# Router logits of three row tiles in one group of matmuls, a second expert computed with seven block products, and shorter pauses in the last routing

## Chip, cores and metric

The kernel runs on one core of one Trainium2 chip. The metric is the device time of one execution in microseconds (us), lower is better. The engines are named as in the profile: PE is TensorE (PEld its weight loads), DVE is VectorE, ACT is ScalarE, POOL is GpSimd, SP is SyncE, whose instructions here only start transfers.

## What is computed

Block-sparse attention with 4 batches, 8 heads, 768 positions and 64 values a head, in blocks of 32 (each query block sees its neighbours, the first and the last block, and three sampled ones; the first and last query blocks see all). Its 3072 x 512 output is the input of a mixture of 8 experts, of which each row takes the best two:

```python
logits = x @ w_gate
noise_scale = np.log1p(np.exp(x @ w_noise))
noisy_logits = logits + noise_scale * noise
top2 = np.argpartition(-noisy_logits, 2, axis=1)[:, :2]
...                                  # top2_w: softmax over the two
h = np.maximum(x[mask] @ w1[e], 0.0) # w1[e] 512 x 1024
out[mask] += top2_w[mask, k, None] * (h @ w2[e])
```

## The kernel before

**Attention and router.** The attention is cut into steps; most of them ("G") handle one half of the heads of 128 query rows. `Attention.steps` writes the order by hand. A step issues the scores (L215), their row maximum on DVE (L250, L269), the transposes of the step before (L303, copied out by ACT, L305), the exponentials on ACT (L291), the product with the values for the step before that (L318), and its scaling on DVE. Two steps make one tile of 128 finished rows x; there are 24, in four groups of 6.

Between these, `step(n, spot)` puts the router's work. Two steps after a tile is done, `turn_rows` transposes it (L548, four transposes on PE, one DVE copy to `r_xT`); a step later `new_logits` multiplies it with the gate and noise weights (L560: the tile stands in the array, 16 columns stream past, copied out by DVE to `r_lc`, L562). Both stand at spot 1, right behind the L303 transposes, and share one PSUM tile, `pe`, with the routing's matmuls. When a group of 6 tiles has its logits, `Router.run` routes it: a generator of small DVE steps with two sorts of PE work, ranks (L635 to L639) and slot tables (L713). `background` takes steps from it. A `yield 2` ahead of PE work makes the following calls idle, as many as `FENCE` says.

**Experts.** There are nine units: units 0 and 1 are the two row sets of expert 0 (640 and 224 rows), units 2 to 8 are experts 1 to 7 with 816 rows. A unit is a first product and a second product (`mm2`). Weights and activations are split in two float16 parts, so each product is three matmuls. Units below `FAST` = 3 use `mm1` (L987): 8 blocks f, for unit 2 with 24 matmuls of 408 columns each. Units from `FAST` on use `fast1` (L1002): 7 block products in place of 8, 168 matmuls of 408 columns in place of 192. For that the weights need sums (`sums`, L838 and L857) and the transposed rows need sums too (`halves`, L880 and L898). These are made on DVE and ACT during the second product of the unit before (`coming`).

**The last routing** (rows of the last six tiles) runs inside unit 0: `mm1` calls `turn()` in the middle and at the end of each f, `mm2` in the middle and at the end of each chunk of 128 rows, and `turn` is `background(UB)` with `UB` = 20 and `FENCE` = [1, 2]. When it is done, `third()` gathers the rows of units 1 and 2 (L926 on POOL), transposes them by DMA (L942 on SP, to `xtb` for unit 1 and `xta` for unit 2). It goes one stage further per chunk of unit 0's second product.

Engines work in program order, each on its own queue, and wait for each other by semaphores.

## Time and profile before

| | us |
|---|---|
| median of 3 runs (864.75 to 867.81) | 866.12 |
| the profiled execution | 856.92 |
| its span, first to last instruction | 855.1 |
| attention and router, up to unit 0's first product | about 316 |
| unit 0 and unit 1 | 316 to 403.5 |
| unit 2 (expert 1), first product | 403.5 to 436.6 |

A row of the timeline gives start, duration, engine, line, operation, output and inputs, shapes, the count of merged instructions, and in brackets how long the engine sat idle before and what released it. "Issue" stands for a wait that the profile doesn't explain.

### The profile page before, as it was taken

Reading aid. Unit: us, or ns where it says so; the run is one execution under the profiler, and the core shown is the slowest. Engines: PE = TensorE matmul, PEld = TensorE weight load, DVE = VectorE, ACT = ScalarE, POOL = GpSimd, SP = SyncE. Lnnn points to the kernel's source line nnn. Section 1 sums busy time; section 2 is a strip of 40 time slices with the busy share of each in tenths; the row PEclk is TensorE's granted clock in tenths of the full one; section 3 lists DMA queues with packets and bytes.
Section 4 is the critical chain, followed back from the end, with each engine's and each line's share of the span. In section 5 each row is a group of like instructions: output and inputs, shape, how many; then the busy total and the mean of one; then the engine's idle time right before and its main releaser. Section 6 shows DMA issues by size and latency. Waiting matters only on the chain.

```text
span 855.1 us, 21866 instructions
## 1 busy us (share of the span) xinstructions
PE 791.1 (93%) x8889; PEld 483.4 (57%) x8889; DVE 549.3 (64%) x1122; ACT 372.6 (44%) x678; POOL 360.2 (42%) x555
## 2 busy tenths in 40 slices
PE   4899888889898878989999999999999999999996
PEld 2577676666676766548544544544544544544542
DVE  3555475756767845722558688678787786868741
ACT  2575464555565534301435445445435445435400
POOL 2534552542224520051317526537537546546431
PEclk9999898998998989999999999999999999999998
DMA  8856986695259898557845696695696695796221
GB/s 336 296 187 220 267 244 187 240 365 174 75 148 256 237 170 303 207 141 160 188 147 127 135 255 140 121 246 130 149 238 141 148 249 119 131 241 140 76 80 53
DMA packets 125021, 159.71 MB, mean 187 GB/s; under 512 B 66581, under 2 KB 83221, under 8 KB 124912
## 3 DMA queue, kind: packets, MB, share of 16 engines
q1 hardware_dynamic: 96400, 75.76, 32.6%
q0 software_dynamic: 20016, 57.47, 27.1%
q10 hardware_dynamic: 8496, 25.01, 9.3%
q8 instruction: 72, 1.18, 0.6%
q14 instruction: 37, 0.30, 0.1%
HBM read 117.30 MB, written 27.10 MB: 169 GB/s over the span
## 4 chain that ended last, share of the span: by engine, by line
PE 54%; DMA 1%; issue 1%; POOL 0%; DVE 0%; POOLq 0%
PE py L1083 26%; PE mb L1002 9%; PE ma L1002 6%; PE mc L1002 6%; PE ph L987 5%; PE py L1093 2%; DMA xtb<-xg 1%; PE py L1102 0%; DMA xg<-x_rows,gi 0%; POOL out_dram L1159 0%; DMA out_dram<-y,mt 0%; DVE y L1145 0%; PE pr L1114 0%; POOLq L1179 0%; POOLq L926 0%
## 5 line engine op out<-in xcount | busy, mean ns | idle before, releaser
L1133 POOL DMA_INDIRECT pv<-out_dram,gi x42 | 101.9, 2425 | 95.6 <-ACT pv L1127 49.3
L1002 PEld LDWEIGHTS <-wop 128*128 128x128 f16 x1008 | 98.6, 98 | 76.3
L1083 PEld LDWEIGHTS <-hh 128*128 128x128 f16 x768 | 74.5, 98 | 89.7 <-issue 2.5
L215 PE MATMUL s<-kv,q 64*32 64x192 f32 (+3 forms) x1920 | 95.9, 357 | 22.9 <-DMA kv<-in_k_dram 8.5
L305 ACT ACTIVATE t<-t 128x512 f32<-128x512 f32 (+1 forms) x120 | 63.0, 566 | 85.5 <-PE t L303 82.5
L205 POOL COPY kv<-kv 128x128 f32 x264 | 67.7, 305 | 52.9 <-issue 25.1
L1159 POOL DMA_INDIRECT out_dram<-pv,mt x42 | 51.8, 1233 | 89.2 <-DMA out_dram<-pv,mt 35.3
L1002 PE MATMUL mb<-tx,wop 128*128 128x408 f16 x432 | 83.3, 336 | 0.0
L215 PEld LDWEIGHTS s<-kv,q 64*32 64x32 f32 (+2 forms) x1920 | 52.6, 130 | 45.9 <-issue 16.6
L291 ACT ACTIVATE p<-s,nb 128x256 f32<-128x256 f32 x176 | 69.5, 477 | 19.3 <-DVE nb L269 13.8
L250 DVE TENSOR_REDUCE nm<-s 128x4 f32<-128x1024 f32 (+1 forms) x48 | 54.4, 1133 | 32.3 <-PE s L215 32.2
L1083 PE MATMUL py<-w2h,hh 128*128 128x512 f16 x192 | 72.8, 379 | 0.0
L1083 PE MATMUL py<-w1ha,hh 128*128 128x512 f16 x192 | 72.8, 379 | 0.0
L1083 PE MATMUL py<-w2l,hh 128*128 128x512 f16 x192 | 72.8, 379 | 0.0
L1083 PE MATMUL py<-w1la,hh 128*128 128x512 f16 x192 | 72.8, 379 | 0.0
L303 PE MATMUL t<-ident,p 128*128 128x128 f32 x448 | 69.1, 297 | 3.5 <-ACT t L305 3.5
L1083 PE MATMUL py<-w2h,hl 128*128 128x512 f16 x192 | 68.9, 379 | 0.0
L1083 PE MATMUL py<-w1ha,hl 128*128 128x512 f16 x192 | 68.8, 379 | 0.0
L303 PEld LDWEIGHTS t<-ident,p 128*128 128x128 f32 x448 | 51.2, 148 | 28.0 <-issue 15.7
L1007 ACT ACTIVATE hh<-us 128x408 f16<-128x408 f32 x48 | 26.1, 543 | 91.8 <-DVE us L1023 91.8
L926 POOL DMA_INDIRECT xg<-x_rows,gi x56 | 57.9, 1033 | 15.9 <-issue 15.0
L1083 PEld LDWEIGHTS <-hl 128*128 128x128 f16 x384 | 37.6, 98 | 45.3
(213 smaller groups left out, 1465.1 us busy)
## 6 DMA issues: line engine op xcount, KB each, us to landing
wraw<-in_moe_w_dram SPq DMA_DIRECT2D x64, 512.0 KB, 5.3
vb<-in_v_windows_dram ACTq DMA_DIRECT2D x28, 390.0 KB, 6.3
vb<-in_v_windows_dram ACTq DMA_DIRECT2D x14, 520.0 KB, 4.9
kv<-in_v_dram SPq DMA_DIRECT2D x4, 1560.0 KB, 17.8
q<-in_q_dram SPq DMA_DIRECT2D x12, 512.0 KB, 8.0
kv<-in_k_dram SPq DMA_DIRECT2D x8, 768.0 KB, 11.1
out_dram<-zero ACTq DMA_DIRECT2D x8, 768.0 KB, 5.1
x_rows<-x SPq DMA_DIRECT2D x20, 256.0 KB, 3.4
```

Source lines behind the costliest of these rows:

```text
L205: nc.gpsimd.tensor_copy(KG[:, j, :, 32 * s:32 * s + 32], KT[:, :, bass.ds(offs[3 * j + s], 32)])
L215: mm = lambda out, l, r, pos: nc.tensor.matmul(out, l, r, start=True, stop=True, tile_position=pos)
L250: red = lambda out, x: nc.vector.tensor_reduce(out, x, axis=AX.X, op=ALU.max, negate=True)
L291: self.nc.scalar.activation(p[:, 256 * u:256 * u + 256], S[:, a, 256 * r:256 * r + 256], AF.Exp, bias=nb[:, u:u + 1], scale=0.125)
L303: self.nc.tensor.transpose(T[i][:, c:c + P], p[:, i * w + c:i * w + c + P], self.ident)
L305: self.nc.scalar.activation(t[:, i * w:(i + 1) * w], T[i][:, 0:w], AF.Copy)
L926: g = nc.gpsimd.indirect_dma_start(out=self.xg[0:m, c], out_offset=None, in_=self.x_dram[0:nr], in_offset=bass.IndirectOffsetOnAxis(ap=r[" ...
L987: nc.tensor.matmul(ph[:, b, 0:m], w[wt][:, kb, fs], r["xt"][:, kb, a, o:o + m], start=i == 0, stop=i == last)
L1002: self.nc.tensor.matmul(bank[:, 0:H], w[:, h, o, k, cs], x(k, a), start=start and i == 0, stop=i == len(seq) - 1, skip_group_check=True)
L1083: nc.tensor.matmul(py, h[:, f, o], w[x][:, f, :], start=i == 0, stop=i == last)
L1133: g = nc.gpsimd.indirect_dma_start(out=y[0:m], out_offset=None, in_=self.out, in_offset=bass.IndirectOffsetOnAxis(ap=r["gi"][0:m, c:c + 1] ...
L1159: x = self.nc.gpsimd.indirect_dma_start(out=self.out, out_offset=bass.IndirectOffsetOnAxis(ap=self.st["u", u]["mt"][0:m, c:c + 1], axis=0) ...
```

## The change

Three things. (1) For 18 of the 24 tiles the logits of three tiles are computed at once: the weights, filled up to 32 columns, stand in the array, three copies side by side in column tiles, and the three transposed tiles stream past them (12 matmuls, 128 columns each). The result comes out transposed, is copied to `r_lt`, and is transposed back two steps later (`logits_rows`). Grouped are the first 15 tiles and tiles 18 to 20; tiles 15, 16, 17, 21, 22, 23 go one by one as before. All logits of the attention move from spot 1 to spot 2, behind the L318 products; `logits_rows` takes spot 1. (2) `FAST` is 2: unit 2 uses `fast1`. Its weights' sums are made in unit 0's second product, its rows' sums in unit 1. (3) `UB` is 10 and `FENCE` [1, 1] for the last routing, `third()` starts with whichever chunk of unit 0 finds it done, and unit 2's transposes take the chunks gathered first.

```diff
+    def logits_of_three(self, i, pl):
+        nc, KB = self.nc, self.D // P
+        for kb in range(KB):
+            for c in range(LG):
+                nc.tensor.matmul(pl[32 * c:32 * c + 32, 0:P], self.wgn[:, kb], self.xT[i - LG + 1 + c][:, kb],
+                                 start=kb == 0, stop=kb == KB - 1, tile_position=(0, 32 * c), skip_group_check=True)
+        for c in range(LG):
+            del self.xT[i - c]
+        nc.vector.tensor_copy(self.lt[0:32 * LG], pl[0:32 * LG, 0:P])
+
+    def logits_rows(self, i, pl):
+        nc, t = self.nc, i % self.T
+        nc.tensor.transpose(pl[:, 0:P], self.lt, self.ident)
+        nc.vector.tensor_copy(self.logit_tile(i)[:, t - LG + 1:t + 1],
+                              pl[:, 0:32 * LG].rearrange("p (t e) -> p t e", e=32)[:, :, 0:2 * E])
...
-        self.FAST = 3
+        self.FAST = 2
...
+    def grouped(i):
+        return i // T < B - 2 or i % T < T - LG
...
-    UB = 20
+    UB = 10
...
         if spot == 1:
+            logits_rows(n)
+            turn_rows(n)
+        if spot == 2:
             new_logits(n)
-            turn_rows(n)
...
-    FENCE[:] = [1, 2]
+    FENCE[:] = [1, 1]
...
         for i in range(ex.count(2)):
-            ex.xpose(2, i)
+            ex.xpose(2, (i + ex.count(1)) % ex.count(2))
...
     for u in range(nu):
         if u == 2:
             turns.close()
-            ex.open_third(hidden)
-        if u == ex.FAST:
             hidden.close()
...
-                ex.split_piece(*((0, 4 + f) if f < 4 else (1, f - 4)))
+                if f < 4:
+                    ex.split_piece(0, 4 + f)
...
-            if u == 2 and f < 4:
-                ex.split_piece(e, 4 + f)
+            if u == 1:
+                for i in {5: (0,), 6: (1,), 7: (2, 3)}.get(f, ()):
+                    ex.halves(2, i)
+            if u == 2 and f % 2 == 0:
+                ex.split_piece(e, 4 + f // 2)
...
-                if k < 4:
+                if k == n - 1:
+                    for _ in rest:
+                        pass
+                if k == 0:
+                    ex.sums_open(1)
+                for i in {0: ((0, 0),), 1: ((0, 1), (0, 2)), 2: ((0, 3), (1, 0)), 3: ((1, 1), (1, 2)), 4: ((1, 3),)}[k]:
+                    ex.sums(1, *i)
+                if k < 2:
                     ex.load_piece(1, 4 + k)
-            if u == 1:
-                for _ in range(3):
-                    next(rest, None)
+            if u == 1 and k == 0:
+                for i in range(6, 8):
+                    ex.load_piece(1, i)
+                for i in range(4, 6):
+                    ex.halves(2, i)
```

Where instructions move, three places. First PE in the attention, the step whose logits are those of the third tile; t are transposes, po the value products, s the next scores. Before:

```order
L303 MATMUL t_1419<-ident,p 128x128 x4
L560 MATMUL pe<-r_wgn,r_xT 128x16 x4
L318 MATMUL po<-va_87,t 32x65 x4
...
L318 MATMUL po<-vb_89,t 32x65 x4
L215 MATMUL s<-kv_85,q 128x64 x4
L215 MATMUL s<-kv_85,q 32x2x96 x16
```

Now (the new lines are `logits_of_three`, L576, and two steps later `logits_rows`, L585):

```order
L304 MATMUL t_1409<-ident,p 128x128 x4
L319 MATMUL po<-va_87,t 32x65 x4
...
L319 MATMUL po<-vb_89,t 32x65 x4
L576 MATMUL pe<-r_xT,r_wgn 32x128 x12
L216 MATMUL s<-kv_85,q 128x64 x4
...
L304 MATMUL t_1649<-ident,p 128x128 x4
L585 MATMUL pe<-r_ident,r_lt 128x128
L319 MATMUL po<-va_87,t 32x65 x4
```

The logits leave the place between the transposes and the value products; in two of three such steps nothing takes it, in the third the group stands behind the value products.

Second DVE around unit 1, whose first product leaves the hl pieces of 224 columns and whose outputs are the y rows behind them. Before:

```order
L1125 TENSOR_SCALAR y<-py,r_tab 128x512 x2
L993 SCALAR_TENSOR_TENSOR hl<-ph,hh 128x224 x8
L906 TENSOR_SCALAR mt<-r_tab 128x7
L912 TENSOR_SCALAR gi<-mt 128x7
L1125 TENSOR_SCALAR y<-py,r_tab 128x512
L1125 TENSOR_SCALAR y<-pr,r_tab 96x512
L993 SCALAR_TENSOR_TENSOR hl<-ph,hh 128x408 x2
```

Now (L895 are the rows' sums of unit 2, L1008 the hl, L1140 the y, L1038 the first addition of unit 2's `fast1`):

```order
L1008 SCALAR_TENSOR_TENSOR hl<-ph,hh 128x224 x6
L895 TENSOR_TENSOR xg<-xta 128x1632
L1008 SCALAR_TENSOR_TENSOR hl<-ph,hh 128x224
L895 TENSOR_TENSOR xg<-xta 128x1632
L1008 SCALAR_TENSOR_TENSOR hl<-ph,hh 128x224
L895 TENSOR_TENSOR xg<-xg 128x2x408 x4
L895 TENSOR_TENSOR tx<-xg,tx 128x1632 x2
L921 TENSOR_SCALAR mt<-r_tab 128x7
L927 TENSOR_SCALAR gi<-mt 128x7
L1140 TENSOR_SCALAR y<-py,r_tab 128x512
L1140 TENSOR_SCALAR y<-pr,r_tab 96x512
L1038 TENSOR_TENSOR r_xT<-mb,r_xT 128x408
```

The rows' sums of unit 2 stand between the last hl pieces of unit 1 and behind them.

Third POOL at unit 0's second product: the scatters of its chunks (out_dram<-y) and the gathers of units 1 and 2 (xg). Before:

```order
L1159 DMA out_dram<-y,mt 3072x512 x3
L926 DMA xg<-x_rows,gi 128x1024
L926 DMA xg<-x_rows,gi 96x1024
L926 DMA xg<-x_rows,gi 128x1024 x4
L926 DMA xg<-x_rows,gi 48x1024
```

Now:

```order
L1174 DMA out_dram<-y,mt 3072x512
L941 DMA xg<-x_rows,gi 128x1024
L941 DMA xg<-x_rows,gi 96x1024
L941 DMA xg<-x_rows,gi 128x1024 x4
L941 DMA xg<-x_rows,gi 48x1024
```

The gathers stand behind the first chunk's scatter instead of the third's.

## Rows read from the trace of the kernel before

**Rows 1.** The chain that ended last: start, us, what; pieces from 403 to 472.
```profile
403.50 33.12 PE ph L987 x192
...
470.51 1.04 PE ma L1002 x6
```
**Rows 2.** Timeline of PEld: a step with neither turn nor logits.
```profile
55.18 0.86 PEld L303 LDWEIGHTS t<-ident,p 128*128 128x128 f32 x8 [0.30 <-ACT p L291]
56.20 0.16 PEld L318 LDWEIGHTS po<-va,t 128*32 128x32 f32 x8 [0.17 <-issue]
```
**Rows 3.** The same view: steps with logits, with a turn, and the next transposes.
```profile
77.46 0.86 PEld L303 LDWEIGHTS t<-ident,p 128*128 128x128 f32 x8 [0.30 <-issue]
...
79.28 0.16 PEld L318 LDWEIGHTS po<-va,t 128*32 128x32 f32 x8
...
80.33 1.10 PEld L215 LDWEIGHTS s<-kv,q 64*128 64x128 f32 x40
81.73 0.86 PEld L303 LDWEIGHTS t<-ident,p 128*128 128x128 f32 x8 [0.30 <-ACT p L291]
...
83.19 0.16 PEld L318 LDWEIGHTS po<-va,t 128*32 128x32 f32 x8 [0.17 <-issue]
...
91.93 0.64 PEld L303 LDWEIGHTS t<-ident,p 128*128 128x128 f32 x6 [0.30 <-issue]
```
**Rows 4.** Timeline of ACT: last exponentials before the transposes at 81.73 and 91.93.
```profile
80.62 0.84 ACT L291 ACTIVATE p<-s,nb 128x256 f32<-128x256 f32 x2
...
89.84 1.20 ACT L291 ACTIVATE p<-s,nb 128x256 f32<-128x256 f32 x3
```
**Rows 5.** Timeline of PE: routing matmuls that waited for a logits copy.
```profile
171.62 1.60 PE L713 MATMUL pe<-r_val,r_hot 128*128 128x126 f32 x12 [0.87 <-DVE r_lc L562]
204.45 0.18 PE L635 MATMUL pe<-r_O,r_tri 128*128 128x48 f16 x1 [0.61 <-DVE r_lc L562]
292.17 1.60 PE L713 MATMUL pe<-r_val,r_hot 128*128 128x126 f32 x12 [1.44 <-DVE r_lc L562]
```
**Rows 6.** Timeline: the longest wait of PE inside value products.
```profile
131.47 0.33 PE L318 MATMUL po<-va,t 128*32 128x65 f32 x3 [4.12 <-issue]
```
**Rows 7.** Timeline of PE: unit 0's first product and first slot table.
```profile
340.34 0.70 PE L987 MATMUL ph<-xta,w1ha 128*128 128x320 f16 x4 [3.46 <-DVE hl L993]
...
353.11 1.60 PE L713 MATMUL pr<-r_val,r_hot 128*128 128x126 f32 x12 [1.04 <-DVE r_val L707]
354.55 0.38 PE L1083 MATMUL py<-w2h,hh 128*128 128x512 f16 x1
```
**Rows 8.** Timeline of DVE: the last routing's pieces in unit 0.
```profile
335.09 0.45 DVE L585 RECIPROCAL r_iw<-r_w 128x48 f32<-128x48 f32 x1
...
337.84 0.15 DVE L607 TENSOR_TENSOR r_dl<-r_mx 128x6 f32<-128x6 f32 x1
...
347.46 0.24 DVE L642 TENSOR_TENSOR r_A<-r_A,pr 128x96 f32<-128x96 f32 x1
...
350.28 0.17 DVE L684 TENSOR_SCALAR r_sl<-r_s 128x12 int32<-128x12 f32 x1
```
**Rows 9.** Timelines of PE, POOL and SP: unit 1's start, gathers and DMA transposes.
```profile
384.33 0.37 PE L987 MATMUL ph<-xtb,w1ha 128*128 128x224 f16 x2 [2.38 <-DMA xtb<-xg]
373.95 1.05 POOL L926 DMA_INDIRECT xg<-x_rows,gi  x1 [0.30 <-DVE gi L912]
375.30 0.97 POOL L926 DMA_INDIRECT xg<-x_rows,gi  x1 [0.31 <-issue]
390.14 10.29 SPq L942 DMA_TRANSPOSE xta<-xg  x7
```
**Rows 10.** Groups by line: shapes and count | busy us, mean ns of one | idle.
```profile
L880 DVE TENSOR_TENSOR xg<-xta 128x1632 f32<-128x1632 f16 x6 | 11.1, 1850 | 3.5 <-DMA xta<-xg 3.5
L880 DVE TENSOR_TENSOR xg<-xg 128x816 f32<-128x816 f32 x24 | 24.1, 1005 | 0.4
L898 ACT ACTIVATE tx<-xg 128x1632 f16<-128x1632 f32 x12 | 18.6, 1553 | 0.0
```

More of the change, by code (lines that the diff above doesn't have):

```diff
@@ L36 @@
 NSLOT = NV * OVC
+LG = 3
 BIGIDX = 1 << 20
@@ L484, in consts @@
         nc, pool, T, B, KB = self.nc, self.pool, self.T, self.B, self.D // P
-        wgn = self.wgn = pool.tile([P, KB, 2 * E], F32, name="r_wgn")
+        wgn = self.wgn = pool.tile([P, KB, 32], F32, name="r_wgn")
+        nc.vector.memset(wgn[:, :, 2 * E:], 0.0)
         nc.sync.dma_start(wgn[:, :, 0:E], w_gate.rearrange("(k p) e -> p k e", p=P))
-        nc.sync.dma_start(wgn[:, :, E:], w_noise.rearrange("(k p) e -> p k e", p=P))
+        nc.sync.dma_start(wgn[:, :, E:2 * E], w_noise.rearrange("(k p) e -> p k e", p=P))
         self.noise = pool.tile([P, B, T, E], F32, name="r_noise")
@@ L514, in tables @@
         nc.vector.tensor_scalar(self.tokf, self.tok, float(-BIGIDX), None, op0=ALU.add)
+        self.lt = pool.tile([P, P], F32, name="r_lt")
+        nc.vector.memset(self.lt, 0.0)
         self.tab = pool.tile([P, NV * NC, 2], F32, name="r_tab")
@@ L548, in turn, with logit_tile @@
             nc.tensor.transpose(pt[:, kb * P:(kb + 1) * P], xv[:, kb * P:(kb + 1) * P], self.ident)
-        self.xT[i] = self.pool.tile([P, self.D // P, P], F32, name="r_xT", bufs=2)
+        self.xT[i] = self.pool.tile([P, self.D // P, P], F32, name="r_xT", bufs=4)
         nc.vector.tensor_copy(self.xT[i].rearrange("p k r -> p (k r)"), pt)
+    def logit_tile(self, i):
+        b = i // self.T
+        if b not in self.lc:
+            self.lc[b] = self.pool.tile([P, self.T, 2 * E], F32, name="r_lc", bufs=2)
+        return self.lc[b]
     def logits(self, i, pl):
-        nc, T, KB = self.nc, self.T, self.D // P
-        b, t = divmod(i, T)
-        if t == 0:
-            self.lc[b] = self.pool.tile([P, T, 2 * E], F32, name="r_lc", bufs=2)
+        nc, KB = self.nc, self.D // P
         xT = self.xT.pop(i)
         for kb in range(KB):
-            nc.tensor.matmul(pl[:, 0:2 * E], xT[:, kb], self.wgn[:, kb], start=kb == 0, stop=kb == KB - 1,
+            nc.tensor.matmul(pl[:, 0:2 * E], xT[:, kb], self.wgn[:, kb, 0:2 * E], start=kb == 0, stop=kb == KB - 1,
                              skip_group_check=True)
-        nc.vector.tensor_copy(self.lc[b][:, t], pl[:, 0:2 * E])
+        nc.vector.tensor_copy(self.logit_tile(i)[:, i % self.T], pl[:, 0:2 * E])
+    def logits_of_three(self, i, pl):
+        nc, KB = self.nc, self.D // P
+        for kb in range(KB):
[10 more added lines that the diff above has]
+                              pl[:, 0:32 * LG].rearrange("p (t e) -> p t e", e=32)[:, :, 0:2 * E])
     def run(self, b, ps):
@@ L810, in open_first @@
     def open_first(self, e):
-        KB, F = self.KB, self.F
-        n = KB * F
-        if e == 0:
-            h, l = (self.wpa.tile([P, n], F16, name=x) for x in ("w1ha", "w1la"))
-        else:
-            both = self.sums_tile()
-            h, l = both[:, 0:n], both[:, n:2 * n]
-        view = lambda t: t.rearrange("p (k f) -> p k f", k=KB)
+        h, l = (self.wpa.tile([P, self.KB * self.F], F16, name=x) for x in ("w1ha", "w1la"))
+        view = lambda t: t.rearrange("p (k f) -> p k f", k=self.KB)
         self.wb[e] = {"w1h": view(h), "w1l": view(l)}
@@ L861, in sums @@
             self.sums_split(e, s, 0, top)
-            s3 = self.st["s3", e, s] = self.tsp.tile([P, 2, 256], F32, name="s3", bufs=2)
+            s3 = self.st["s3", e, s] = self.tsp.tile([P, 2, 256], F32, name="s3", bufs=1)
             tt(s3, a11, a21, ALU.subtract)
@@ L938, in xpose @@
         r = self.st["u", u]
-        if c == 0:
+        if "xt" not in r:
             pool, x = (self.xta, "a") if u % 2 == 0 else (self.xtb, "b")
@@ L1043, in fast1 @@
             mul(A, 0, plain(0, 0), True)
-            m = new("um", 2)
+            m = self.router.pool.tile([P, 4, P], F32, name="r_xT", bufs=4).rearrange("p k r -> p (k r)")[:, 0:H]
             nc.scalar.activation(m, A[:, 0:H], AF.Copy)
             mul(B, 2, mixed(1, 1), True)
-            s2 = self.router.pool.tile([P, 4, P], F32, name="r_xT", bufs=2).rearrange("p k r -> p (k r)")[:, 0:H]
+            s2 = self.router.pool.tile([P, 4, P], F32, name="r_xT", bufs=4).rearrange("p k r -> p (k r)")[:, 0:H]
             add(s2, B[:, 0:H], m)
@@ L1299, in turn_rows, with begin, logits_rows @@
             fresh.append((n + 1, i))
+    def grouped(i):
+        return i // T < B - 2 or i % T < T - LG
+    def begin(i):
+        if i % T == T - 1:
+            jobs.append(router.run(i // T, lambda: psum[0]()))
+            started[0] += 1
     def new_logits(n):
         while fresh and fresh[0][0] <= n:
+            i = fresh.pop(0)[1]
+            if grouped(i) and i % LG < LG - 1:
+                continue
             while router.held:
                 background()
-            i = fresh.pop(0)[1]
-            router.logits(i, psum[0]())
-            if i % T == T - 1:
-                jobs.append(router.run(i // T, lambda: psum[0]()))
-                started[0] += 1
+            if grouped(i):
+                router.logits_of_three(i, psum[0]())
+                turned.append((n + 2, i))
+            else:
+                router.logits(i, psum[0]())
+                begin(i)
+    def logits_rows(n):
+        while turned and turned[0][0] <= n:
+            while router.held:
+                background()
+            i = turned.pop(0)[1]
+            router.logits_rows(i, psum[0]())
+            begin(i)
     psum = [att.psum]
@@ L1434, in coming @@
         e = ex.units[u][1]
-        if u + 1 < ex.FAST:
-            return
         if k == 0:
```

4 lines of the change are left out of this document (1 added, 3 removed).

## Prediction

> **What bounds the kernel now.** I read the chain that ended last first. From 384.33 us, where unit 1 waits for a DMA transpose [rows 9], it follows PE alone to the last output, and unit 2's first product takes 33.12 us of it [rows 1]. So from there on PE's own work is the time. In the attention I read the timeline of weight loads, which shows when PE takes up each piece. PE goes from one piece to the next with no gap but a fixed 0.30 us ahead of each run of transposes [rows 2, 3]. So the attention is bound by PE as well, with two conditions. The gap is sometimes released by ACT's exponentials, so ACT is close behind. And PE has long waits that no instruction explains, 4.12 us at the longest [rows 6]; with it there are six above 1.4 us in the attention. They won't shrink because a matmul is gone.
>
> **Part 1, the logits.** From the start of a run of transposes to the value products a step takes 56.20 - 55.18 = 1.02 us with nothing between [rows 2], 79.28 - 77.46 = 1.82 with logits, and 83.19 - 81.73 = 1.46 with a turn [rows 3]. So one tile's logits cost 0.80 us and one transpose of 128 x 128 costs 0.44 / 4 = 0.11.
>
> A group of 12 new matmuls isn't in the trace. Nearest are the value products: 64 records (32 matmuls, each in a 32-column tile, four side by side) take 80.33 - 79.28 = 1.05 us [rows 3], so a set of four with 65 columns takes 0.131. Scaled to 128 columns that is 0.26, times four sets 1.03 us. The lower bound is the streaming of 128 columns at the transposes' rate, 0.86 / 8 = 0.108 us a record [rows 3], two records to a float32 matmul, four sets: 0.86 us. The upper bound is no overlap of the column tiles, 24 x 0.108 = 2.6 us. I take 1.0, since the value products show the overlap in this very form.
>
> Per group: two tiles' logits go (1.60), the third's 0.80 becomes 1.0, and a transpose comes (0.11): 1.3 us, times six groups 7.8. That the third tile's step gives no more is important. The transposes at 81.73, behind the third tile's logits, were released by ACT, whose exponentials ended at 80.62 + 0.84 = 81.46; behind the fourth's they ended at 91.04, 0.9 before the transposes at 91.93 [rows 3, 4]. So the steps that lose work have about 0.9 us of room on the side of ACT, those that get the group have little.
>
> Routing matmuls that waited for a logits copy, 0.87, 0.61 and 1.44 us [rows 5], no longer follow one. But three of them now follow a group, and must wait for DVE's copy of it: three times about 0.6, as in the middle one of these rows. That is +1.1 us. The wider copy and the copy back replace three copies of 0.17 us on DVE and hide beside PE.
>
> Two single tiles (17 and 21) now stand apart from the transposes, whose array shape they share. The trace shows 0.30 and 0.17 us at changes of shape [rows 2, 3], but none between logits and value products, so I count nothing. The Trainium skill, in "TensorEngine Tiling (Array Packing)", section Tiling Modes, says that every change of the tiling mode drains TensorE. By it the two tiles would cost 0.47 us each and the saving would be 0.9 smaller.
>
> Sum 8.9 us on PE. I take 6 of it (two thirds), because ACT, DVE and the unexplained waits give some back; bounds 2 (all that stands before a long wait is lost) and 9.
>
> **Part 2, the last routing.** Its calls pause less: one idle call behind a `yield 2` and not three, and at most ten steps at once. On PE the ranks (L635) come ahead of f = 5, the first slot table ahead of f = 7, the second in the middle of the first chunk. The wait of 3.46 us [rows 7] stays: PE needs hl of f = 3 and now also the ranks' inputs, and DVE makes both behind 2.75 us of routing from 335.09 on [rows 8], about 1 us for the rest; f = 5 starts near 340.5 as before (340.34) [rows 7]. The first table then is needed too early. DVE goes: hl of f = 4 until 344.2; L642 to L682, 350.28 - 347.46 = 2.8 us [rows 8], until 347.0; hl of f = 5 until 348.5; L684 until the table's inputs, 353.11 - 350.28 = 2.8 [rows 7, 8], until 351.3. PE has finished f = 6 at 348.8 (f = 5 and 6 take 8.3), so it waits 2.5 us, and the second product starts near 356.0 in place of 354.55 [rows 7]: 1.5 us lost. In return nothing waits later. The second product takes 27.2 us as before (five chunks and the second table) and ends at 383.2; the gathers start near 365 and not 373.95, and what took 384.33 - 375.30 = 9.0 us from the second gather to unit 1's start [rows 9] is over by 376. So the 2.38 us wait goes and unit 1 starts at about 383.2, 1.1 us earlier. After the 3.46 us wait f = 5 took 5.0 us where others take 3.3, at a granted clock below full; a second such fall would cost 1.7. I take +0.5, bounds -0.6 and +2.5.
>
> **Part 3, unit 2 by seven products.** 192 matmuls in 33.12 us become 168: 28 pieces of six at 1.035 us, 28.97 us [rows 1]. Gain 4.15. Its weights' sums lie on DVE and ACT in unit 0's second product, where DVE is idle most of the time, and cost nothing: at most 4.9 us of chain per chunk of 5.18. The rows' sums lie tighter. With t the end of f = 5 in unit 1 (f takes 1.17 us): hl of f = 5 until t + 1.1, a sum of 1.85 us [rows 10], hl of f = 6, a sum of 1.85, hl of f = 7 at t + 5.2. PE ends f = 7 at t + 2.3 and needs the last hl at t + 3.2, near the end of the first of four column blocks of the next product. It waits about 2 us, 2.3 with f = 6. Then four sums of 1.0 us, two ACT pieces of 1.55 and two DVE pieces of 1.86 [rows 10] end at t + 14.7, and PE comes to the second product of unit 2 at about t + 15.5. That is just in time. So -2.3, bounds -4 and -0.5. Unit 2's w2 splits join the seven products as in later units, with one more of 1.2 us on DVE; no cost.
>
> **Sum.** 6 + 0.5 + 4.15 - 2.3 = 8.3 us. The profiled execution took 856.92 us (span 855.1), 9.2 below the median 866.12; I carry the difference over: span 846.8, median 857.8.
>
> **Rivals.**
> *The attention gives nothing* (ACT's chain and the long waits absorb it): for it speaks that ACT releases the transposes in the third tile's step [rows 3]; against, the 0.9 us of room in the others. Gain 2.3, 863.8.
> *Column tiles one after the other*: each group 2.6 us, 6 x 1.6 = 9.6 us more than in the sum, 867.4. Against it stand the value products.
> *Everything hides*: the routing's wait before f = 7 is covered, hl isn't delayed: 6 + 2.5 + 4.15 - 0.5, 854.0.
> *Slower: DVE stuck on the row sums.* `halves` for unit 2 waits for seven DMA transposes. If the gathers come so late that these start as before, 5.8 us after unit 1's start, and take 10.29 us [rows 9] and some 3 to land, DVE sits from f = 5 on with hl of f = 6 and 7 behind it. Then unit 2 starts 19 + 13 us after unit 1 in place of 19: 13 lost. With the attention's middle gain that is 866.12 - 6 - 0.5 - 4.15 + 13 = 868.5, at its low end 872.5. It decides when the last transpose lands later than about 7 us after unit 1's start; I expect it 3 us or more after the second product's end at most, near 386 to 388 against a limit of 390.
> *The change doesn't do what it says*: the order of instructions shows all three parts in place.
>
> **How the numbers follow.** Forecast 0.6, all faster. Everything hides 0.16, faster. Attention gives nothing 0.13: half of it faster by over 0.3% (2.6 us, about what a measurement can tell from no change), half the same. Column tiles in turn 0.05, the same. DVE stuck 0.06, slower by 0.05, the same 0.01. Together faster 0.82, same 0.13, slower 0.05. The range reaches from everything hidden with a little more (853.5) to the attention giving nothing (864.5).
>
> **What would show it.** Right: value products about 1.0 us behind each run of transposes in the steps that lost logits; L576 rows of 0.9 to 1.1 us; no wait on xtb at unit 1; a wait of about 2.5 us before the first slot table; one of about 2 us in unit 1's second product on hl; 29 us for unit 2's first product. Wrong: PE gaps on ACT's exponentials of more than 0.5 us in those steps, L576 near 2.6, or DVE rows of L895 that wait for xta.

## The result and the profile after

The changed kernel takes 873.75 us (median of 20 runs), the kernel before beside it 864.54 us (20 runs): ratio 1.0088, 95% interval 1.0063 to 1.0112. The ratios here and below compare fast executions alone, so they aren't the quotients of the medians beside them, and the changed kernel's profiled execution is one of its five slow ones. The change costs 0.88% of 864.54, 7.6 us, where I had forecast a gain of 8.3. The profiled execution took 876.95 us, 3.2 above its median, and the one of before (856.92) 7.6 below the median here; so of the 20 us between the two traces only about 8 belong to the change, and I read single places of the traces, not their ends.

The page of the changed kernel: span, busy time of each engine, and the chain that ended last by engine.

```profile
span 875.1 us, 21889 instructions
PE 794.4 (91%) x8871; PEld 476.1 (54%) x8871; DVE 577.6 (66%) x1158; ACT 380.6 (43%) x688; POOL 362.5 (41%) x556
...
PE 69%; DVE 12%; issue 6%; DMA 3%; ACT 3%; POOL 2%; SPq 2%; POOLq 1%; another core or an unknown queue 0%; ACTq 0%; DVEq 0%
```

PE still holds most of the chain, but waits now lie between its pieces. The timeline of PE, from unit 0 to unit 2's start (start, duration, engine, line, operation, tiles, shapes, count, idle time before and its releaser):

```profile
349.72 0.20 PE L660 MATMUL pr<-r_O,r_tri 128*128 128x48 f16 x1 [3.30 <-DVE r_O L645]
360.15 1.67 PE L738 MATMUL pr<-r_val,r_hot 128*128 128x126 f32 x12 [3.36 <-DVE r_val L732]
...
397.72 0.35 PE L1002 MATMUL ph<-xtb,w1ha 128*128 128x224 f16 x2 [1.50 <-DVE hl L1008]
...
406.88 0.20 PE L1117 MATMUL py<-hl,w2h 128*128 128x96 f16 x1 [1.29 <-DVE hl L1008]
408.95 0.20 PE L1117 MATMUL py<-hl,w2h 128*128 128x96 f16 x1 [1.78 <-DVE hl L1008]
...
421.14 1.20 PE L1017 MATMUL ma<-xta,wop 128*128 128x408 f16 x6 [1.67 <-DVE y L1140]
```

The 3.46 us wait of [rows 7] is there as forecast (3.30, now ahead of the ranks), the new one ahead of the slot table is 3.36 us where I had 2.5, and the wait on xtb ahead of unit 1 [rows 9] is gone. The three kinds in unit 1 are the news: 1.50 us in its first product, 1.29 and 1.78 in its second, 1.67 ahead of unit 2.

Two tables hold what follows. They are worked out from timelines: the starts of PE's first matmul of each product, and in the attention the starts of DVE's 64 score reductions (L250, after the change L251), numbered from 1. First the experts, in us:

| kernel | unit 0, both products | unit 1, first | unit 1, second | unit 2, both |
|---|---|---|---|---|
| before | 67.6 | 9.21 | 9.79 | 67.0 |
| e16, before again | 65.1 | 13.10 | 9.79 | 67.0 |
| changed | 67.1 | 10.86 | 16.52 | 64.5 |
| e9, changed again | 64.2 | 12.62 | 20.20 | 64.5 |
| e3, changed without part 1 | 70.3 | 13.46 | 16.38 | 64.5 |
| e4, changed without part 2 | 69.8 | 12.01 | 18.76 | 64.5 |
| e7, load behind | 67.6 | 9.33 | 14.60 | 64.5 |
| e10, sums that wait for nothing | 66.8 | 10.58 | 13.46 | 64.4 |
| e11, both mends | 63.4 | 10.76 | 13.66 | 64.5 |

Then the attention, us between reductions:

| kernel | 1 to 31 | 31 to 45 | 45 to 52 | 52 to 63 | 63 to 64 |
|---|---|---|---|---|---|
| before | 136.7 | 70.3 | 23.54 | 58.7 | 3.45 |
| e6, before with late routing | 131.6 | 71.0 | 29.49 | 59.0 | 3.46 |
| e1, before with part 1 | 133.1 | 70.7 | 29.52 | 59.8 | 3.83 |
| changed | 130.9 | 72.8 | 29.55 | 60.2 | 11.13 |
| e5, part 1 mended | 129.2 | 68.8 | 25.39 | 59.3 | 3.82 |

Two places carry the loss: unit 1, 8.4 us longer (27.38 for 19.00), and the stretch from reduction 45 to 52, 6.0 us longer (4.4 to 7.0 in the seven kernels traced with part 1 as changed). Of the 8.4 only the 6.7 in the second product is clearly the change's: this product takes 9.79 us in all ten traces without part 3 and 13.46 to 20.20 in the ten with it, but the first product took 13.10 in the kernel before itself when it was traced again (e16). The last column is another matter (see the end).

### The profile page after: what moved, and what is told of

It reads as the page before. It is cut to its first block, busy times and chain, and to the rows that moved or that the text cites. A ratio compares the mean times of both kernels' runs of the same rounds, so it can differ in the third digit from the quotient of the medians.

```text
span 875.1 us, 21889 instructions
## 1 busy us (share of the span) xinstructions
PE 794.4 (91%) x8871; PEld 476.1 (54%) x8871; DVE 577.6 (66%) x1158; ACT 380.6 (43%) x688; POOL 362.5 (41%) x556
## 4 chain that ended last, share of the span: by engine, by line
PE 69%; DVE 12%; issue 6%; DMA 3%; ACT 3%; POOL 2%; SPq 2%; POOLq 1%; another core or an unknown queue 0%; ACTq 0%; DVEq 0%
PE py L1098 27%; PE mb L1017 9%; PE mc L1017 7%; PE ma L1017 7%; PE s L216 5%; PE po L319 4%; PE t L304 3%; PE py L1108 2%; DVE nm L251 2%; PE ph L1002 2%; SPq L957 2%; POOL kv L206 2%; DMA kv<-in_k_dram 2%; PE pe L738 1%; DMA va<-in_v_dram,vidx 1%
## 5 line engine op out<-in xcount | busy, mean ns | idle before, releaser
L1017 PEld LDWEIGHTS <-wop 128*128 128x128 f16 x1176 | 115.5, 98 | 96.6 <-issue 9.0
L1148 POOL DMA_INDIRECT pv<-out_dram,gi x42 | 93.4, 2224 | 105.2 <-ACT pv L1142 61.1
L216 PE MATMUL s<-kv,q 64*32 64x192 f32 (+3 forms) x1920 | 100.7, 358 | 24.3 <-DMA kv<-in_k_dram 8.5
L1017 PE MATMUL mb<-tx,wop 128*128 128x408 f16 x504 | 98.5, 337 | 3.6 <-DVE us L1038 3.4
L206 POOL COPY kv<-kv 128x128 f32 x264 | 70.7, 317 | 53.2 <-issue 22.5
L1174 POOL DMA_INDIRECT out_dram<-pv,mt x42 | 55.5, 1322 | 85.1 <-DMA out_dram<-pv,mt 33.6
L251 DVE TENSOR_REDUCE nm<-s 128x4 f32<-128x1024 f32 (+1 forms) x48 | 54.3, 1132 | 38.6 <-PE s L216 28.5
L304 PE MATMUL t<-ident,p 128*128 128x128 f32 x448 | 71.1, 303 | 4.9 <-ACT t L306 4.7
L1022 ACT ACTIVATE hh<-us 128x408 f16<-128x408 f32 x56 | 30.4, 543 | 103.4 <-DVE us L1038 89.5
L1098 PE MATMUL py<-w2h,hh 128*128 128x512 f16 x192 | 72.8, 379 | 0.0
L1098 PE MATMUL py<-w1ha,hh 128*128 128x512 f16 x192 | 72.8, 379 | 0.0
L1098 PE MATMUL py<-w2l,hh 128*128 128x512 f16 x192 | 72.8, 379 | 0.0
L1098 PE MATMUL py<-w1la,hh 128*128 128x512 f16 x192 | 72.8, 379 | 0.0
L941 POOL DMA_INDIRECT xg<-x_rows,gi x56 | 60.9, 1087 | 15.7 <-issue 15.7
L1174 POOL DMA_INDIRECT out_dram<-y,mt x14 | 14.7, 1048 | 122.3 <-DVE mt L921 65.1
```

Of the source, the lines that this page charges most:

```text
L206: nc.gpsimd.tensor_copy(KG[:, j, :, 32 * s:32 * s + 32], KT[:, :, bass.ds(offs[3 * j + s], 32)])
L216: mm = lambda out, l, r, pos: nc.tensor.matmul(out, l, r, start=True, stop=True, tile_position=pos)
L251: red = lambda out, x: nc.vector.tensor_reduce(out, x, axis=AX.X, op=ALU.max, negate=True)
L304: self.nc.tensor.transpose(T[i][:, c:c + P], p[:, i * w + c:i * w + c + P], self.ident)
L941: g = nc.gpsimd.indirect_dma_start(out=self.xg[0:m, c], out_offset=None, in_=self.x_dram[0:nr], in_offset=bass.IndirectOffsetOnAxis(ap=r[" ...
L1017: self.nc.tensor.matmul(bank[:, 0:H], w[:, h, o, k, cs], x(k, a), start=start and i == 0, stop=i == len(seq) - 1, skip_group_check=True)
```

## The experiments

All ratios are to the kernel before, run beside on the same chip.

| run | what | median us | before us | ratio (95%) |
|---|---|---|---|---|
| e1 | part 1 alone | 860.48 | 858.83 | 1.0029 (0.9993 to 1.0064) |
| e2 | part 2 alone | 857.59 | 858.83 | 1.0003 (0.9968 to 1.0037) |
| e3 | parts 2 and 3 | 863.02 | 858.83 | 1.0053 (1.0018 to 1.0088) |
| e4 | parts 1 and 3 | 869.48 | 858.83 | 1.0116 (1.0077 to 1.0156) |
| e5 | part 1 mended | 855.26 | 859.27 | 0.9941 (0.9920 to 0.9962) |
| e6 | late routing alone | 864.07 | 859.27 | 1.0042 (1.0009 to 1.0076) |
| e7 | changed, load behind | 860.41 | 859.27 | 1.0019 (0.9992 to 1.0047) |
| e8 | changed, sums of unit 1's rows | 862.83 | 859.27 | 1.0027 (0.9994 to 1.0060) |
| e9 | changed again | 871.76 | 865.16 | 1.0085 (1.0040 to 1.0129) |
| e10 | e8 with a buffer of its own | 872.37 | 865.16 | 1.0110 (1.0054 to 1.0166) |
| e11 | changed, both mends | 861.12 | 865.16 | 0.9967 (0.9933 to 1.0001) |
| e12 | parts 1 (mended) and 2 | 861.68 | 865.16 | 0.9975 (0.9939 to 1.0011) |
| e13 | e11, outputs on ACT | 862.22 | 867.14 | 0.9950 (0.9914 to 0.9985) |
| e14 | e13, outputs in a free buffer | 863.77 | 867.14 | 0.9984 (0.9944 to 1.0023) |
| e15 | e5 again | 866.05 | 867.14 | 0.9994 (0.9955 to 1.0034) |
| e16 | before again | 863.76 | 865.47 | 0.9982 (0.9945 to 1.0019) |
| e17 | e5 without the last group | 863.09 | 865.47 | 0.9957 (0.9915 to 0.9998) |
| e18 | e5, third time | 859.60 | 865.47 | 0.9949 (0.9914 to 0.9985) |

### Which part loses: e1 to e4

e1 takes over the new logits alone; e2 is two numbers:

```diff
-    UB = 20
+    UB = 10
...
-    FENCE[:] = [1, 2]
+    FENCE[:] = [1, 1]
```

e3 is the changed kernel with `grouped` returning False and the logits back at spot 1; e4 is the changed kernel with the two numbers above as before.

> The kernel before with part 1 alone: logits of three tiles at once, put after the products in the step (the tiles' buffer and the two buffers that it takes from the experts' code move with it); unit 2 still by the plain products, last routing as before. Theory A (the loss sits in the attention: in the two profiles unit 0 starts 9.8 us later, 326.5 for 316.7): slower than before, +4 to +10 us. Theory B (the attention gains as forecast or nothing, and the profiles' 9.8 us are the spread between one fast and one slow execution): -6 to 0 us. My forecast of part 1 was -6.

> The kernel before with part 2 alone: at most ten steps of the last routing at once and one idle call less. Forecast -0.5 us (bounds -2.5 to +0.6); by what the changed kernel's trace shows (a wait of 3.30 us ahead of the ranks and one of 3.36 us ahead of the first slot table, where I had 3.46 and 2.5) +0.5 to +2 us, unless an earlier start of unit 1 gives it back. Theory A says that it matters little, theory B that it and part 3 together cost 8 us or more.

> The changed kernel with part 1 undone: single logits at their old place, last routing and seven products as changed. Theory A: -2 to -3 us against the kernel before, as forecast (0.5 + 4.15 - 2.3). Theory B: +4 to +10 us, with the waits of unit 1's second product on hl and unit 2's wait for the rows' sums in the trace as in the changed kernel.

> The changed kernel with part 2 undone: twenty steps of routing at once and the idle calls as before; logits of three and seven products stay. If part 2 costs nothing here, the changed kernel's time (+7 to +9 us against the kernel before); if the routing has to be early so that the gathers, the transposes and unit 2's row sums come in time, +12 us or more; if part 2's new waits are the loss, within 4 us of the kernel before.

Neither theory holds alone. e1 and e3 lose 0.29% and 0.53% (e1's interval just takes in no loss), together 0.82%, near the change's 0.88%: as far as the intervals tell, two losses that add. Part 2 alone is worth nothing measurable. Without it the changed kernel is no better (1.0116): unit 1 then waits 5.05 us for xtb at its start, and its second product is 18.76 us long.

### Part 1: e5 and e6

e5 puts the group where the single logits stood and its turn back into the same step, so that the routing starts as early as before; e6 leaves the logits alone and starts the routing of the first two batches two steps later.

```diff
         if spot == 1:
-            logits_rows(n)
+            new_logits(n)
             turn_rows(n)
         if spot == 2:
-            new_logits(n)
+            logits_rows(n)
...
-                turned.append((n + 2, i))
+                turned.append((n, i))
```

```diff
-                jobs.append(router.run(i // T, lambda: psum[0]()))
-                started[0] += 1
+                delayed.append((n + (2 if i < 2 * T else 0), i))
+        while delayed and delayed[0][0] <= n:
+            i = delayed.pop(0)[1]
+            jobs.append(router.run(i // T, lambda: psum[0]()))
+            started[0] += 1
```

> Part 1 alone again, but the three tiles' logits stand at the place of the single ones and their turn back in the same step, so that the routing of the first two batches starts as early as before and not two steps later. Theory R (PE does save its 8.9 us, but the routing that starts later falls with its pieces into steps where VectorE and ScalarE are late already, which gives it all back between 152 and 237 us): the attention ends 4 to 7 us earlier than with the logits as changed, the time is 854 to 857 us where the kernel before has 858.8. Rival S (the saved matmuls were never on the path, the steps being bound by ScalarE and VectorE): within 1.5 us of the logits as changed (860.5 us).

> The kernel before with one thing only: the routing of the first two batches starts two steps later; single logits, nothing saved on PE. Theory R: the trace has the longer waits around its second slot table near 220 to 237 us, and the attention is 5 to 9 us longer, so +4 to +8 us in all. Rival S: within 1.5 us of the kernel before, since a later routing then costs nothing.

Theory R holds on both sides. The late start alone costs 3.6 us (e6; its interval is 0.8 to 6.5), and removing it turns part 1 from 2.5 us lost into 5.1 us won on the same chip. (e5 also moves the group ahead of the value products, so it doesn't single out the start; e6 does.) The second table shows the place: 29.5 us from reduction 45 to 52 in e6, which saves nothing on PE, as in e1. How it comes about stands in the timeline of e1 (DVE, then ACT, then PE):

```profile
227.25 1.04 DVE L726 TENSOR_TENSOR r_hot<-r_io,r_pm 128x768 f32<-128x768 f32 x1
228.22 0.64 DVE L730 TENSOR_TENSOR r_val<-r_eq,r_tokf 128x378 f32<-128x378 f32 x1
228.78 0.64 DVE L732 TENSOR_TENSOR r_val<-r_eq,r_pay 128x378 f32<-128x378 f32 x1
229.74 0.89 DVE L367 TENSOR_TENSOR xr<-po,rc 128x128 f32<-128x128 f32 x3
230.66 0.63 ACT L379 ACTIVATE x<-xr 128x512 f16<-128x512 f32 x1 [1.89 <-DVE xr L367]
231.20 0.85 ACT L306 ACTIVATE t<-t 128x384 f32<-128x384 f32 x2
231.72 1.54 PE L304 MATMUL t<-ident,p 128*128 128x128 f32 x6 [2.21 <-ACT t L306]
...
237.63 0.65 PE L552 MATMUL pe<-r_ident,xr 128*128 128x128 f32 x4 [1.27 <-DVE r_tab L741]
```

Three pieces of the second slot table stand in DVE's queue ahead of xr, the scaling of finished rows. ACT's conversion of xr waits 1.89 us, ACT's copy of the transposed exponentials stands behind that conversion, and PE waits 2.21 us for the copy. e6 has the same two waits to the hundredth:

```profile
229.29 0.63 ACT L378 ACTIVATE x<-xr 128x512 f16<-128x512 f32 x1 [1.89 <-DVE xr L366]
...
230.35 1.43 PE L303 MATMUL t<-ident,p 128*128 128x128 f32 x6 [2.21 <-ACT t L305]
```

The 6.0 us of the table aren't all a cost of the late start. The stretch runs between DVE's reductions, and e6 does 50 more of PE's matmuls in it. These are its windows in the kernel before and in e6; a row has the window, its length, the busy time and count of PE, PEld, DVE, ACT and POOL, then the granted clock, the DMA share and GB/s:

```profile
217.80:241.40 23.60, 21.59 (x378) 15.63 (x378) 15.09 (x42) 12.74 (x28) 7.09 (x18) 1.00 0.40 114
213.40:242.90 29.50, 24.77 (x428) 18.74 (x426) 18.67 (x53) 13.55 (x29) 8.19 (x18) 0.94 0.33 93
```

Besides its waits e6 has a granted clock of 0.94 there: the slot table right behind the 2.21 us wait takes 2.63 us where the one before took 1.60.

```profile
231.58 2.63 PE L713 MATMUL pe<-r_val,r_hot 128*128 128x126 f32 x12
```

So the price of the late start is e6's 3.6 us and not 6.0. In e5 the pieces come earlier and delay little; PE's wait for the copy in that step is 0.31:

```profile
225.96 0.93 PE L304 MATMUL t<-ident,p 128*128 128x128 f32 x6 [0.31 <-ACT t L306]
```

### Part 3: e7, e8 and e10

In the changed kernel these rows tell of the seven transposes of xta: the first gather (POOL), a weight load (SP) right behind unit 1's transposes, all seven transposes behind it in SP's queue, the last two of them again by themselves, and DVE's first row sum, which waits for them.

```profile
376.15 1.13 POOL L941 DMA_INDIRECT xg<-x_rows,gi  x1 [0.30 <-issue]
382.55 1.09 SPq L824 DMA_DIRECT2D wraw<-in_moe_w_dram  x1
383.81 18.88 SPq L957 DMA_TRANSPOSE xta<-xg  x7
400.01 2.68 SPq L957 DMA_TRANSPOSE xta<-xg  x2
404.67 1.86 DVE L895 TENSOR_TENSOR xg<-xta 128x1632 f32<-128x1632 f16 x1 [1.37 <-DMA xta<-xg]
```

e7 moves the load (piece 5 of expert 1) behind the transposes. e8 makes unit 2's sums from unit 1's rows; e10 also writes them into the free buffer `pv`.

```diff
-                if k < 2:
+                if k < 1:
                     ex.load_piece(1, 4 + k)
             if u == 1 and k == 0:
-                for i in range(6, 8):
+                for i in range(5, 8):
```

```diff
-            x = r["xt"][:, 2 * d:2 * d + 2]
+            x = (self.st["u", 1] if u == 2 else r)["xt"][:, 2 * d:2 * d + 2]
...
-        X = self.xg.rearrange("p c d -> p (c d)").bitcast(F32)[:, 0:4 * C].rearrange("p (d k c) -> p d k c", d=2, k=2)
+        flat = self.pv if u == 2 else self.xg.bitcast(F32)
+        X = flat.rearrange("p c d -> p (c d)")[:, 0:4 * C].rearrange("p (d k c) -> p d k c", d=2, k=2)
```

> The changed kernel with one weight load (the sixth piece of expert 1, 1 MB in the queue of the transposes) put behind unit 2's DMA transposes. Theory Q (this load waits for a buffer until 382.55 in the changed kernel's trace, and the seven transposes of xta stand behind it in SP's queue): the first transpose starts up to 4 us earlier, the last lands 2 to 4 us earlier against unit 1's start, and unit 2 starts 2 to 4 us earlier. Rival T (the transposes are slow because the DMA engines are full with gathers and scatters): their last landing stays about 28 us behind the first gather, time as the changed kernel's (+7 to +8 us against before).

> The changed kernel with unit 2's row sums made from unit 1's rows, which are turned early (unit 2's result is therefore not the reference's); the same instructions, but the sums no longer wait for the late transposes. If the late transposes are what makes unit 1's second product long (16.5 us where it had 9.8): it falls to 12 to 13 us, and unit 2 starts 3 to 4.5 us earlier. If VectorE's work alone is too long there, as much as the landing: under 1.5 us.

> As the changed kernel, but unit 2's row sums are made from unit 1's rows and written into the buffer of unit 2's outputs, which nothing uses yet (unit 2's result is not the reference's). In the earlier try they still waited, since they overwrite the buffer that the transposes read. If the late transposes make unit 1 long: its two products take 21 to 23 us in place of 27.4, as my forecast had it (2.3 over 19.0), and unit 2 starts 4 to 6 us earlier. If VectorE's own work is enough to do it: 25 us or more.

> The changed kernel itself, on the same chip as the next three, for a second trace and for ratios on one chip. +5 to +9 us against the kernel before. The steps of the attention should have the lengths of the first trace (6.5, 1.3, 2.6, 6.8, 4.5, 2.7 us between the score reductions 45 to 51), and unit 1's two products should take 27 us together again where the kernel before has 19.0; the single value product of 6.88 us behind the last step but one should not come again if it was chance.

e7: the first transpose moves from 7.7 us behind the first gather to 6.6, by the load's own 1.09 us in the queue (it's 0.5 MB by the page and not 1, and no row shows the wait for a buffer that I had in theory Q), the last lands 26.7 us behind it and not 28.5, and unit 1 takes 23.93 us and not 27.38, so 3.45 us less. Little of that is the wait for the transposes, which is still 0.96 us where it was 1.29:

```profile
393.46 0.20 PE L1117 MATMUL py<-hl,w2h 128*128 128x96 f16 x1 [0.96 <-DVE hl L1008]
```

1.5 us are the wait in the first product, which e7 hasn't, and 1.6 a granted clock that stayed up (both below). The ratio falls by more, but the two ratios come from different chips.

e8 told nothing on its question. Its first sum still waits for the transposes, although it reads xtb, because it overwrites the buffer that they read:

```profile
394.72 1.86 DVE L895 TENSOR_TENSOR xg<-xtb 128x1632 f32<-128x1632 f16 x1 [0.89 <-DMA xta<-xg]
```

e10 removes that too. Unit 1 takes 24.04 us: 3.3 less than in the first trace of the changed kernel, 8.8 less than in e9, and 1 us more than I had set as the upper bound. Three waits stay:

```profile
398.53 0.35 PE L1003 MATMUL ph<-xtb,w1ha 128*128 128x224 f16 x2 [1.22 <-DVE hl L1009]
...
408.29 0.20 PE L1118 MATMUL py<-hl,w2h 128*128 128x96 f16 x1 [1.77 <-DVE hl L1009]
...
418.88 1.20 PE L1018 MATMUL ma<-xta,wop 128*128 128x408 f16 x6 [1.67 <-DVE y L1141]
```

So the late transposes are one part, and 5 us are there without them. What they cost directly is the wait for them, 1.29 us in the first trace and this in e9:

```profile
400.95 0.24 PE L1117 MATMUL py<-hl,w2h 128*128 128x96 f16 x1 [4.73 <-DVE hl L1008]
```

The time doesn't show e10's gain: its ratio is not under e9's, with intervals of about 0.5% each way and an attention that differed by 10 us between the two traces. What I say of e10 rests on the trace of unit 1 alone.

### Both mends, and the two other waits: e11 to e15

e11 joins e5's and e7's edits in the changed kernel; e12 is e5 with e2's two numbers. e13 adds to e11 that unit 1's outputs leave PSUM on ACT, e14 that unit 0's outputs go to `pv`, so that none waits for a scatter.

```diff
+        if u == 1:
+            nc.scalar.activation(y[0:m], py[0:m, 0:D], AF.Copy, scale=w[0:m, c:c + 1])
...
-        y = self.pv[:, c] if 2 <= u < len(self.units) - 1 else self.yp.tile([P, D], F32, name="y")
+        y = self.pv[:, c] if u == 0 or 2 <= u < len(self.units) - 1 else self.yp.tile([P, D], F32, name="y")
```

> The changed kernel with both mends: logits of three at the place of the single ones with their turn in the same step, and the weight load behind unit 2's transposes. If the two losses are separate, the gains add: 6 to 8 us for the first and 3 to 5 for the second, so 4 to 7 us under the kernel before. If they overlap, about as the load alone (+1 us).

> The kernel before with the mended logits and the last routing as changed, without the seven products. Against the kernel before -4 to -6 us, as the mended logits alone (last routing alone was worth nothing). If it is faster than the kernel with both mends and the seven products, these cost more in unit 1 (8.4 us; about 5 with the load behind) than they give in unit 2 (2.6); I expect it 1 to 3 us faster.

> Both mends, and unit 1's outputs leave PSUM on ScalarE instead of VectorE. In every trace with the seven products unit 2's first product waits 1.67 us for such an output, which stands behind the last pieces of the row sums in VectorE's queue. If that is a cost of its own: this wait is gone, unit 1's two products take 22.5 to 23 us (24.42 with both mends, 24.04 with sums that wait for nothing), and the time is 1.7 us under that of both mends. If the pieces of the row sums themselves are as late, the wait is put down to them and the time stays.

> As the run before it, and unit 0's outputs go into a buffer that is free until unit 2, so that none waits for a scatter to free one of three. In the traces with the seven products hl of unit 1's first product comes 1.2 to 3.3 us late, behind an output of unit 0 that waited for a scatter. If that is the cause: no wait in unit 1's first product (9.2 us), another 1.2 to 1.5 us gained. If the weights' sums on VectorE are the cause, the wait stays.

> Part 1 mended alone, once more, beside the two above on one chip: -4 to -6 us against the kernel before. With the two causes above removed the seven products should gain 0.5 to 3 us on it; if they do not, they are worth nothing in this kernel.

e9 and e11 ran on one chip: the two mends take the changed kernel from 1.0085 to 0.9967, 10 us. e12 without the seven products stands at 0.9975: with unit 1 as it is, they give nothing measurable.

In e13 the wait ahead of unit 2 falls from 1.67 to 0.91 us, but unit 1's second product becomes longer (14.50 for 13.66). The windows of 3 us behind the 1.78 us wait say why. First e7:

```profile
395.60:398.60 3.00, 3.00 (x73) 3.00 (x73) 2.90 (x4) 0.00 (x0) 1.25 (x1) 1.00 0.28 102
```

The same in the changed kernel:

```profile
409.00:412.00 3.00, 3.00 (x43) 3.00 (x43) 2.90 (x4) 0.00 (x0) 0.45 (x1) 0.56 0.13 49
```

And in e13:

```profile
399.20:402.20 3.00, 3.00 (x40) 3.00 (x40) 2.90 (x4) 0.00 (x0) 1.68 (x1) 0.50 0.03 10
```

At a granted clock of 0.56 and 0.50 (the lower level, 1.2 GHz, for all or most of it) PE does 43 and 40 matmuls where it does 73 at full clock. From the end of that wait to ACT's copy of the chunk (L1121) it's 413.89 - 408.95 = 4.9 us in the changed kernel and 398.87 - 395.52 = 3.35 in e7, so the fall costs 1.6 us. In e7, e10 and e11 the clock stayed at 1.00 behind this wait, in the seven other traces with part 3 it was 0.50 to 0.63 there; why it falls in some executions stays open.

In e14 the wait in unit 1's first product is still 1.34 us. So it isn't the scatter. DVE's rows ahead of that hl in e14 show an output, then a piece of the weights' sums, which itself waits for ACT:

```profile
385.63 0.74 DVE L1142 TENSOR_SCALAR pv<-py,r_tab 128x512 f32<-128x512 f32 x1
386.83 1.22 DVE L853 SCALAR_TENSOR_TENSOR wop<-wraw,wop 128x1024 f16<-128x1024 f32 x1 [0.46 <-ACT wop L852]
387.98 0.68 DVE L1008 SCALAR_TENSOR_TENSOR hl<-ph,hh 128x224 f16<-128x224 f32 x2
```

What delays this hl stays open. e7 has the same pieces of the weights' sums, its outputs wait for PE alone, and hl comes in time. In e14 an output of unit 0 waited 3.11 us for something that the profile doesn't name, and the sums fell behind. And two kernels without part 3 have such a wait in this product too, first the kernel before (e16), then e15:

```profile
389.58 0.35 PE L987 MATMUL ph<-xtb,w1ha 128*128 128x224 f16 x2 [2.06 <-issue]
392.86 0.53 PE L1012 MATMUL ph<-xtb,w1ha 128*128 128x224 f16 x2 [2.61 <-DVE hl L1018]
```

e5, e13, e17 and e18 are faster than the kernel before, by 0.4 to 0.6% with intervals that leave out 1, but e15, the same kernel as e5, isn't. e13 is the only one of them with all three parts; e11 and e13 to e15 can't be ranked by their times.

### Is the last column the logits' doing: e16 to e18

e17 is e5 with single logits for tiles 18 to 20; e16 is the kernel before.

```diff
-        return i // T < B - 2 or i % T < T - LG
+        return i // T < B - 2 or i // T == B - 2 and i % T < T - LG
```

> The kernel before itself, for a trace on the chip of the next two. On one chip (e1 to e8) the last value products of the attention took 3.5 to 3.8 us from one score reduction to the next in every kernel; on the other chips of this study (the first trace of the changed kernel, e9 to e15) they took 10.5 to 11.1 us, and all kernels traced there have the three tiles' logits. If it is the chip: about 10.5 us here too, where the next two show it. If it is the logits: 3.5 us here.

> Part 1 mended with five groups: the tiles 18 to 20, whose group stands behind exactly these value products, get single logits again (1.3 us more on PE). If that group, or the buffers it holds, stretches the value products ahead of it: 3.5 us there, and the time 3 to 5 us under the run below. If not: as the run below, or 1 us more.

> Part 1 mended alone, on the chip of the two above: a third measurement after -5 and -0.5 us against the kernel before on two chips. Where its value products take 10.5 us, I expect -2 to 0 us; where they take 3.8 us, -4 to -6.

The long form doesn't need the logits: from reduction 63 to 64 the kernel before takes 8.20 us on this chip, e17 9.51, e18 9.06. So the group of tiles 18 to 20 isn't the cause, and part 1 as a whole has about 1 us of it (one trace each). In these traces the form goes with the chip; the chip of the first two traces isn't on record. My link between this stretch and the gain of the mended logits fell too, since e18 gains 0.51% with it.

## Why the prediction was wrong, point by point

**Part 1** failed at the step that wasn't there: I costed the matmuls and named where the three tiles' result is turned back, "two steps later", but never asked what else starts two steps later. The group itself is as forecast: its 24 records take 1.05 us, with the value products' last at 77.24 right ahead, so the column tiles do overlap and that rival is out.

```profile
77.24 0.29 PE L319 MATMUL po<-vb,t 128*32 128x65 f32 x8
77.36 1.05 PE L576 MATMUL pe<-r_xT,r_wgn 128*32 128x128 f32 x24
```

The steps that lost logits are shorter: between reductions 11 and 12 it's 4.02 to 4.04 us in the three kernels with part 1 as changed (e1, e4, the change) and 5.02 without. With the routing in its old place the gain is 5.1, 0.5 and 4.4 us (e5, e15, e18; 859.27 x 0.0059, 867.14 x 0.0006, 865.47 x 0.0051), 3.3 on average, inside my bounds of 2 to 9 and below the 6 that I took. As changed it's -2.5 (interval -5.5 to +0.6): the late routing, a term that my sum didn't have, costs 3.6 us by itself (e6) and shows between reductions 45 and 52. My reason for taking two thirds (ACT and DVE give some back) named the right engines, but not the mechanism.

**Part 2** isn't contradicted: +0.5 forecast, 0 +/- 3 measured (e2). The waits were 3.30 and 3.36 us in the changed kernel; the second, for which I had 2.5, runs from 1.46 to 5.32 in the other traces with part 2. The wait on xtb went, and the second product took 27.23 us as forecast.

**Part 3, the gain.** 28.97 us forecast for the first product by seven products; later units take 28.98 (26.91 and a tail of 2.07). Unit 2 takes 28.03 + 2.06 = 30.1, since PE waits there three times some 0.4 us for DVE (L1038), each time behind a piece of the weights (L853). With the second product, which starts 0.5 us later behind the tail, both take 64.5 for 67.0: 2.5 us gained where I had 4.15.

**Part 3, the stall** is the term that decided: 2.3 us forecast (bounds 0.5 to 4), 8.4 measured, of which 6.7 in the second product. What I had in the sum, DVE's own work ahead of hl, is the 1.78 us wait. Beside it stand four that I had at nothing:
- The late transposes: 1.29 us of wait in the first trace, 4.73 in e9. I let the transposes land 3 to 5 us behind unit 1's start, near 386 to 388 for a gather at 365, so some 22 us. They land 28.5 us behind the first gather (33.7 in e9), in the kernel before 28.5 too (the last is issued at 399.15 and lands 3.3 us later, the median of the seven; 402.5 - 373.95). My figure took the 10.29 us of [rows 9] as the transposes' own time and let the gathers run beside them. That doesn't go: while almost nothing else ran, from 390 to 403 in the kernel before, the packets of the transposes' queue alone took 87% of the time of the 16 DMA engines.
- The rival that I gave 0.06, DVE stuck on late transposes, is this very mechanism: the last lands 10.9 us behind unit 1's start (404.67 - 393.76) where I had put the limit at 7. Its price was 13 us; the wait for the transposes is 1.29 us in one trace and 4.73 in the other. (Against e10, whose sums wait for nothing, unit 1 is 3.3 and 8.8 us longer, but the clock and the first product differ as well.)
- The fall of the clock behind the waits, 1.6 us.
- The output that leaves PSUM behind the row sums in DVE's queue, a wait of 1.67 us (0.91 with the output on ACT). I had counted the sums until t + 14.7 and PE's arrival at t + 15.5 as "just in time", without the output that stands behind the sums.
- hl in unit 1's first product, 1.50 us. The last piece of the weights' sums, which I had "cost nothing" in unit 0's second product, stands ahead of it, but in e7 it costs nothing, and e15 and e16 wait 2.61 and 2.06 us without these sums. So this part isn't shown to be the change's.

With 0.5 us left over that makes 8.4 (1.78 + 1.29 + 1.6 + 1.67 + 1.50 + 0.5).

The queues of the DMA engines, kernel before from 373 to 390 and from 390 to 403 us (packets, MB, share of 16 engines):

```profile
q0 software_dynamic: 830, 2.65, 50.3%
q1 hardware_dynamic: 2384, 1.05, 25.9%
...
q1 hardware_dynamic: 7392, 1.84, 87.0%
```

The changed kernel from 376 to 390 and from 390 to 405, where gathers, scatters and transposes share them:

```profile
q0 software_dynamic: 559, 1.81, 46.7%
q1 hardware_dynamic: 3138, 1.24, 41.6%
...
q1 hardware_dynamic: 6660, 1.69, 73.8%
q0 software_dynamic: 387, 1.24, 39.6%
```

The two stretches are full (88% and 113%, the sum of two queues' packet times). Started 7.7 us behind the first gather and not 16.2 as in the kernel before, the transposes land no earlier behind it.

**Sum.** Part 1 -2.5, part 2 0, part 3 about 5 us lost by these rows (2.5 - 8.4 = -5.9, against 4.5 by e3): 7 to 8 us lost, and 7.6 measured. That it fits so well is partly luck: 1.7 of the 8.4 us lie in the first product, which differs by 3.9 us between two traces of the kernel before, and e1's and e3's intervals are some 3 us wide each way.

## What to carry to other kernels

When a result comes later by a step or two, price everything that starts from it, on the engines where its pieces land: moved by two steps, work that was free stood ahead of a scaling in an in-order queue and cost about 3.6 us by itself, and part 1 was no gain any more. When a chain of transfers must be early, add up the DMA engines' time of all that runs with it and not only the chain's own. Of instructions put "beside other work" look at what stands behind them in the same queue: PE waited 1.67 us for an output of 0.75 us behind the row sums.

## What the runs showed of the hardware that I hadn't expected

Seven DMA transposes of 128 x 1024 two-byte elements (1.84 MB) have packet times that add up to all 16 DMA engines for 0.87 x 13 = 11.3 us, 1.6 us each, or 163 GB/s. The Trainium skill, in "DMA: Bandwidth & Descriptors", section Latency and other measured facts, gives 261 GB/s for a transpose with a non-contiguous middle dimension; this trace shows less.

The value products ahead of the last group of logits take 3.5 to 3.8 us from reduction 63 to 64 in all kernels traced on the chip of e1 to e8, and 8.2 to 11.1 us on those of e9 to e18, the kernel before included. In the long form PE stops for some 0.4 us after every few matmuls, released by nothing that the profile names, as here in the kernel before (e16):

```profile
302.27 0.26 PE L318 MATMUL po<-vb,t 128*32 128x65 f32 x2 [0.41 <-issue]
302.99 0.35 PE L318 MATMUL po<-va,t 128*32 128x65 f32 x5 [0.37 <-issue]
...
306.64 0.27 PE L318 MATMUL po<-vb,t 128*32 128x65 f32 x1 [1.06 <-issue]
```

The medians of the kernel before differ in the same way, 858.8 and 859.3 us there and 865.2 to 867.1 on the others. What makes the stops stays open.
